# Bulk-load buffers moved to the front of SBUF, each row at a multiple of 512 bytes, in a one-token attention and MLP block

## Chip, cores, metric

One core of one Trainium2 chip. The metric is the device time of one execution in microseconds, as the median of several executions; a profile of one execution lies beside them.

## The reference

A decode step: layer norm of x, sliding-window attention over cached keys and values (8 KV heads, 4 query heads for each, window of 1024 keys, head size 128), an output projection, and a gated MLP branch.

```python
B, Sq, D = 4, 1, 512;  Hq, Hkv, Sk, Dh = 32, 8, 4096, 128;  F = 1792
W = min(4096, max(256, Sk // 4))                       # 1024 keys
q = (xn @ wq).reshape(B, Sq, Hq, Dh).transpose(0, 2, 1, 3)
k = repeat(k_cache[:, :, Sk - W:, :], 4, axis=1)       # v likewise
p = softmax(einsum("bhqd,bhkd->bhqk", q, k) * Dh ** -0.5)
s = einsum("bhqk,bhkd->bhqd", p, v).transpose(...).reshape(B, Sq, Hq * Dh) @ wo
g = silu(gelu(layernorm(xn) @ w1 + b1) @ w2 + b2)
return x + s * g
```

Everything that has to come from HBM (K and V windows, wq, wo, w1, w2) is 28.84 MB of bf16.

## The kernel before

All bulk loads are issued by SP (SyncE) on one DMA queue, queue 1 in the profile, in the order K0, K1, wq (two), K2 to K7, V0, w1, V1, w2, V2 to V7, wo (six pieces). The V loads reuse the K slots of kv_buf and wait for the transposes that read them. PE (TensorE) transposes K, computes scores, P times V, the MLP and the output projection as the loads land. The parts that matter here:

```python
sb = nc.alloc_sbuf_tensor              # buffers follow each other in this order, in steps of 32 B
x_bf = sb([4, 512], BF16)
x16 = sb([16, 128], BF16)
# ... some 20 small buffers cut ...
xyT = sb([128, 32], BF16)
wq_sb = sb([128, 4, HQ * DH], BF16)
qT = sb([128, 128], BF16)
w1_sb = sb([128, 4, F], BF16)
b1_sb = sb([1, F], BF16)
w2_sb = sb([128, FC, D], BF16)
b2_sb = sb([1, D], BF16)
wo_sb = sb([128, HKV, 4, D], BF16)
# ... cut ...
kv_buf = sb([128, NS, NC, DH], BF16)   # 8 slots of 8192 B per partition
kt_buf = sb([128, NKT, UT * 128], BF16)
P_buf = sb([128, HKV, NC * 16], BF16)

def load_v(g):
    d_v[g] = pg.dma("sp", "v%d" % g, lambda e: e.dma_start(
        kv_buf[:, (HKV + g) % NS, :, :].rearrange("p c d -> p (c d)"), cache_rows(A_v_cache, g)),
        t_last[(HKV + g) % NS] if HKV + g >= NS else None)

# the last work: the output projection, piece by piece as wo lands
def wo(k, rows):
    g0, g1, i0, i1, d = d_wo[k]
    # ... for g, i, c: matmul(psM[...], wo_sb[:, g, i, c*128:(c+1)*128], OW[:, i, g*4:(g+1)*4])
    return add("pe", fn, d, rows, mlp["g"])
```

The softmax here doesn't subtract the row's maximum and nothing guards it: scores larger than these inputs give would overflow.

Of the kernel before, what the change touches and what calls it, by code (L numbers as in the profile page):

```python
# [73 lines left out]
def bass_recurrent_scan__sliding_block_cached__mixer_channel_mlp__decode_kernel(  # L74
# [17 lines left out]
    BF16 = dt.bfloat16  # L92
    F32 = dt.float32

    B, D = 4, 512
    HQ, HKV, DH = 32, 8, 128
# [3 lines left out]
    F = B_w1.shape[1]  # L100
    FC = F // 128
    NC = 32
    KR = W // NC
    UT = 8
    NU = NC // UT
    NS = 8
    LAG = 8
    NKT = LAG + 2
# [5 lines left out]
    NEG = -30000.0  # L114

    sb = nc.alloc_sbuf_tensor
    x_bf = sb([4, 512], BF16)
    x16 = sb([16, 128], BF16)
    x32 = sb([4, 512], F32)
# [20 lines left out]
    negm = sb([128, 512], BF16)  # L140

    xyT = sb([128, 32], BF16)
    wq_sb = sb([128, 4, HQ * DH], BF16)
    qT = sb([128, 128], BF16)
    w1_sb = sb([128, 4, F], BF16)
    b1_sb = sb([1, F], BF16)
    w2_sb = sb([128, FC, D], BF16)
    b2_sb = sb([1, D], BF16)
    wo_sb = sb([128, HKV, 4, D], BF16)
    sel = sb([128, 4, 32], BF16)  # L150
    OW = sb([128, 4, HKV * 4], BF16)
    hT = sb([128, FC * 4], BF16)

    kv_buf = sb([128, NS, NC, DH], BF16)
    kt_buf = sb([128, NKT, UT * 128], BF16)
    P_buf = sb([128, HKV, NC * 16], BF16)
    OTb = sb([128, HKV * 16], BF16)
    den_sb = sb([128, HKV * 16], F32)
    rden = sb([128, HKV * 16], F32)
# [395 lines left out]
```

## Time and profile before

| | before |
|---|---|
| timed, median of the first 3 runs | 78.89 us (78.83 to 78.99) |
| the execution that was profiled | 77.54 us, span 75.8 us |
| bulk bytes, data packets | 28.84 MB, 3712 |
| busy: PE, VectorE, queue 1 | 74%, 45%, 91.6% of 16 engines |

A profile is read here from the slices (busy tenths in 40 equal parts), then in windows, then along the chain of work that ended last. The lines are in the prediction. Besides the views, I grouped the trace's records of single DMA packets (queue, start, duration, size); those tables are mine and stand in ordinary fences.

### The profile page before, as it was taken

What the parts mean: (1) busy time and instruction counts of PE and PEld (TensorE: products, weight loads), DVE (VectorE), ACT (ScalarE), POOL (GpSimd) and SP (SyncE); (2) the same over time, 40 slices, a digit from 0 to 9 for tenths busy, and PEclk for the clock granted to TensorE, in tenths of its full rate; (3) what the DMA queues carried; (4) which work ended last, traced back from release to release, by engine and by line L of the source; (5) the groups of instructions that cost most, each with busy time, mean ns of one, the idle gap of its engine ahead of it and who ended that gap; (6) DMA issues with size and microseconds to landing.
All of it is one profiled execution on the core that took longest, in us unless ns stands there. A gap on an engine that the chain in (4) does not pass through costs nothing.

```text
span 75.8 us, 2618 instructions
## 1 busy us (share of the span) xinstructions
PE 55.8 (74%) x1212; PEld 52.8 (70%) x1219; DVE 34.3 (45%) x81; ACT 8.4 (11%) x15; POOL 4.3 (6%) x12
## 2 busy tenths in 40 slices
PE   0009995003996989999999499999689979838850
PEld 0009994004995989999999399999489979737730
DVE  0788988000023668999999300000843563440010
ACT  0615200000000030330330351000100000000000
POOL 6970000000000000000000000000000000000000
PEclk9999999855555559999999995555555555555555
DMA  0899999999999999999999999999999999999600
GB/s 2 279 398 411 447 458 424 432 458 385 419 415 419 428 445 411 419 419 430 437 420 433 419 428 389 437 424 419 398 424 415 415 408 419 432 400 412 255 21 2
DMA packets 4214, 29.01 MB, mean 383 GB/s; under 512 B 486, under 2 KB 491, under 8 KB 1644
## 3 DMA queue, kind: packets, MB, share of 16 engines
q1 hardware_dynamic: 4160, 28.84, 91.6%
q8 instruction: 9, 0.15, 0.8%
q10 hardware_dynamic: 44, 0.01, 0.1%
q14 instruction: 1, 0.01, 0.0%
HBM read 28.85 MB, written 0.00 MB: 381 GB/s over the span
## 4 chain that ended last, share of the span: by engine, by line
DMA 44%; PE 31%; SPq 19%; issue 3%; DVE 1%
DMA wo_sb<-in_A_wo_dram 24%; DMA wq_sb<-in_A_wq_dram 20%; PE psK L272 18%; SPq L435 16%; PE psS L291 7%; PE psM L355 5%; SPq L201 2%; SPq L213 1%; PE psS L497 1%; PE psM L467 1%; SPq L206 0%; DVE o_bf L499 0%; DVE sg_sb L493 0%
## 5 line engine op out<-in xcount | busy, mean ns | idle before, releaser
L272 PE MATMUL psK<-ident,kv_buf 128*128 128x128 bf16 x256 | 23.1, 251 | 6.4 <-DMA kv_buf<-in_A_k_cache_dram 5.7
L272 PEld LDWEIGHTS psK<-ident,kv_buf 128*128 128x128 bf16 x256 | 18.7, 114 | 6.5 <-DMA kv_buf<-in_A_k_cache_dram 5.7
L278 DVE COPY kt_buf<-psK 128x1024 bf16<-128x1024 bf16 x32 | 21.1, 689 | 4.6 <-PE psK L272 4.5
L291 PE MATMUL psS<-qT,kt_buf 128*128 128x16 bf16 x256 | 10.6, 171 | 1.7 <-issue 1.4
L291 PEld LDWEIGHTS psS<-qT,kt_buf 128*128 128x128 bf16 x256 | 9.9, 99 | 2.4 <-issue 1.7
L309 PE MATMUL psO<-P_buf,kv_buf 128*128 128x16 bf16 x256 | 8.4, 175 | 0.5 <-issue 0.5
L309 PEld LDWEIGHTS psO<-P_buf,kv_buf 128*128 128x128 bf16 x256 | 8.1, 105 | 0.6 <-issue 0.6
L299 ACT ACTIVATE P_buf<-psS 128x512 bf16<-128x512 f32 x8 | 4.8, 597 | 32.9 <-PE psS L291 32.9
L355 PE MATMUL psM<-xyT,wq_sb 128*128 128x4 bf16 x128 | 3.5, 166 | 4.8 <-DMA wq_sb<-in_A_wq_dram 4.8
L355 PEld LDWEIGHTS psM<-xyT,wq_sb 128*128 128x128 bf16 x128 | 3.5, 104 | 4.8 <-issue 4.8
L373 PE MATMUL psM<-xyT,w_sb 128*128 128x4 bf16 x56 | 5.6, 204 | 0.0
L467 PE MATMUL psM<-OW,wo_sb 128*128 128x4 bf16 x128 | 4.4, 167 | 1.4 <-DMA wo_sb<-in_A_wo_dram 0.5
L467 PEld LDWEIGHTS psM<-OW,wo_sb 128*128 128x128 bf16 x128 | 3.9, 105 | 1.9 <-issue 0.9
L381 DVE TENSOR_SCALAR t_sb<-u_sb 128x56 f32<-128x56 f32 x1 | 0.2, 192 | 10.8 <-ACT u_sb L380 10.8
L318 PE MATMUL psO<-P_buf,ones_bf 128*128 128x128 bf16 x32 | 4.7, 302 | 0.0
L373 PEld LDWEIGHTS psM<-xyT,w_sb 128*128 128x128 bf16 x56 | 4.5, 154 | 0.2
L361 DVE CAST qT<-psM 128x128 bf16<-128x128 f32 x1 | 0.4, 440 | 8.2 <-PE psM L355 8.2
L327 DVE TENSOR_REDUCE den_sb<-psO 128x16 f32<-128x128 f32 x8 | 2.3, 289 | 3.5 <-PE psO L318 3.5
L375 PE MATMUL psM<-ones_bf,b_sb 1*128 1x4 bf16 x14 | 3.0, 215 | 0.0
L400 PE MATMUL psM<-hT,w_sb 128*128 128x4 bf16 x56 | 2.1, 167 | 1.0 <-DVE hT L392 1.0
L318 PEld LDWEIGHTS psO<-P_buf,ones_bf 128*128 128x128 bf16 x32 | 2.8, 128 | 0.0
L400 PEld LDWEIGHTS psM<-hT,w_sb 128*128 128x128 bf16 x56 | 1.8, 105 | 1.3 <-DVE hT L392 1.2
(57 smaller groups left out, 25.1 us busy)
## 6 DMA issues: line engine op xcount, KB each, us to landing
kv_buf<-in_A_k_cache_dram SPq DMA_DIRECT2D x8, 1024.0 KB, 21.5
kv_buf<-in_A_v_cache_dram SPq DMA_DIRECT2D x8, 1024.0 KB, 22.1
wq_sb<-in_A_wq_dram SPq DMA_DIRECT2D x2, 2048.0 KB, 13.2
w_sb<-in_B_w_dram SPq DMA_DIRECT2D x2, 1792.0 KB, 31.4
wo_sb<-in_A_wo_dram SPq DMA_DIRECT2D x3, 1024.0 KB, 24.7
wo_sb<-in_A_wo_dram SPq DMA_DIRECT2D x1, 512.0 KB, 21.6
wo_sb<-in_A_wo_dram SPq DMA_DIRECT2D x2, 256.0 KB, 18.0
x<-in_A_x_dram ACTq DMA_DIRECT2D x2, 2.0 KB
```

Of the source, the lines that this page charges most:

```text
L272: last = pe.transpose(psK[n % NB][:, j * 128:(j + 1) * 128], kv_buf[:, g, u * UT + j, :], ident[:, :])
L278: cp[n] = add("dve", lambda e: e.tensor_copy(kt_buf[:, n % NKT, :], psK[n % NB][:, 0:1024]), t, sc.get(n - NKT))
L291: last = pe.matmul(psS[g % 2][:, c * 16:(c + 1) * 16], kt_buf[:, n % NKT, j * 128:(j + 1) * 128], qT[:, g * 16:(g + 1) * 16], start=False, ...
L299: ex[g] = add("act", lambda e: e.activation(P_buf[:, g, :], psS[g % 2][:, 0:512], AF.Exp, scale=SCALE), sc[n])
L309: last = pe.matmul(pso[:, 0:16], kv_buf[:, (HKV + g) % NS, c, :], P_buf[:, g, c * 16:(c + 1) * 16], start=(c == 0), stop=(c == NC - 1))
L318: last = pe.matmul(pso[:, 128:256], ones_bf[:, :], P_buf[:, g, k * 128:(k + 1) * 128], start=(k == 0), stop=(k == 3))
L355: last = pe.matmul(psM[:, PS_Q + h * 4:PS_Q + (h + 1) * 4], wq_sb[:, c, h * DH:(h + 1) * DH], xyT[:, c * 4:(c + 1) * 4], start=(c == 0), s ...
L373: pe.matmul(o, bass.AP(w1_sb, c * F + k, [[4 * F, 128], [FC, 128]]), xyT[:, 16 + c * 4:16 + (c + 1) * 4], start=(c == 0), stop=False)
L375: last = pe.matmul(o, bass.AP(b1_sb, k, [[F, 1], [FC, 128]]), ones_bf[0:1, 0:4], start=False, stop=True)
L400: pe.matmul(o, w2_sb[:, k, c * 128:(c + 1) * 128], hT[:, k * 4:(k + 1) * 4], start=(k == 0), stop=False)
L435: e.dma_start(wo_sb[:, g0:g1, i0:i1, :], wo_r[:, g0:g1, i0:i1, :]))))
L467: last = pe.matmul(psM[:, PS_W + c * 4:PS_W + (c + 1) * 4], wo_sb[:, g, i, c * 128:(c + 1) * 128], OW[:, i, g * 4:(g + 1) * 4], start=firs ...
```

## The change

Its intent: rows that the bulk loads write should start on 512 B boundaries, in case the DMA engines write such rows faster. In the kernel before, kv_buf starts 384 B past such a boundary, w1, w2 and wo 256 B past, wq on it.

```diff
     sb = nc.alloc_sbuf_tensor
+    pad = sb([1, 192], BF16)
+    kv_buf = sb([128, NS, NC, DH], BF16)
+    wq_sb = sb([128, 4, HQ * DH], BF16)
+    wo_sb = sb([128, HKV, 4, D], BF16)
+    w1_sb = sb([128, 4, F], BF16)
+    w2_sb = sb([128, FC, D], BF16)
+    kt_buf = sb([128, NKT, UT * 128], BF16)
+    P_buf = sb([128, HKV, NC * 16], BF16)
     x_bf = sb([4, 512], BF16)
     # ... and the same seven lines removed further down
```

More of the change, by code (lines that the diff above doesn't have):

```diff
@@ L142, in bass_recurrent_scan__sliding_block_cached__mixer_channel_mlp__decode_kernel @@
     xyT = sb([128, 32], BF16)
-    wq_sb = sb([128, 4, HQ * DH], BF16)
     qT = sb([128, 128], BF16)
-    w1_sb = sb([128, 4, F], BF16)
     b1_sb = sb([1, F], BF16)
-    w2_sb = sb([128, FC, D], BF16)
     b2_sb = sb([1, D], BF16)
-    wo_sb = sb([128, HKV, 4, D], BF16)
     sel = sb([128, 4, 32], BF16)
@@ L152, in bass_recurrent_scan__sliding_block_cached__mixer_channel_mlp__decode_kernel @@
     hT = sb([128, FC * 4], BF16)
-    kv_buf = sb([128, NS, NC, DH], BF16)
-    kt_buf = sb([128, NKT, UT * 128], BF16)
-    P_buf = sb([128, HKV, NC * 16], BF16)
     OTb = sb([128, HKV * 16], BF16)
```

## The prediction

> **What bounds the kernel now.** I read the page's slices first, because moving buffers to other addresses can only act through transfers or through engines, and the slices say which of the two is full.
>
> ```profile
> PE   0009995003996989999999499999689979838850
> ...
> DVE  0788988000023668999999300000843563440010
> ...
> DMA  0899999999999999999999999999999999999600
> ...
> q1 hardware_dynamic: 4160, 28.84, 91.6%
> ```
>
> The 16 DMA engines are at 90% or more from the third slice to the 37th, while PE and DVE have holes. One queue carries practically everything: 28.84 MB in 4160 packets. Next I asked for the same in stretches of my own choice (columns: window, length, busy us of PE, PEld, DVE, ACT and POOL, granted clock, DMA share, GB/s):
>
> ```profile
> 8.00:18.00 10.00, 4.50 (x53) 4.24 (x50) 4.71 (x9) 0.01 (x1) 0.00 (x0) 0.83 0.99 423
> ...
> 24.00:35.00 11.00, 10.35 (x208) 10.16 (x211) 8.24 (x13) 1.79 (x3) 0.00 (x0) 0.80 1.02 427
> 35.00:48.00 13.00, 11.79 (x281) 11.30 (x281) 7.04 (x11) 2.99 (x5) 0.00 (x0) 0.90 1.00 420
> 48.00:62.00 14.00, 13.03 (x273) 12.32 (x274) 4.91 (x22) 0.65 (x3) 0.00 (x0) 0.50 1.01 419
> ```
>
> The DMA share is 0.99 to 1.02 whether PE is half idle (8 to 18) or nearly full. So PE's 90% in the later windows is work that keeps up, not the limit. The chain of waits in order of time then shows how the end is set:
>
> ```profile
> 42.90 2.22 SPq L435
> 45.12 0.04 issue
> 45.16 4.54 SPq L435
> ...
> 54.55 18.07 DMA wo_sb<-in_A_wo_dram
> 72.62 0.04 issue
> 72.67 0.39 PE psM L467 x8
> ```
>
> The last weight load is issued at 54.55 us and lands at 72.62 us: a 256 KB piece needs 18 us only because it stands behind others. The issues before it take 2 to 5 us each, which I read as a queue that is full and lets the issuer in only when room comes free. After the landing there are 8 matmuls, two small VectorE operations, one transpose and the store, about 3.2 us in all.
>
> The sum: the first bulk packet starts 2.22 us into the span, the bulk packets run over 70.03 us (first start to last end in the trace's records of single packets), and some 3.5 us follow: 75.8. The profiled run took 77.54 us as a whole, the timed ones 78.89 in the median. The question is therefore one: do these packets get shorter when they land on multiples of 512 bytes?
>
> [...]
>
> **The change part by part.** It removes and adds no instruction, wait or transfer; only addresses move, plus a 384-byte pad that nothing writes. The compiled program of before lists its addresses: wq starts at 28160 (55 x 512, already aligned), w1, w2 and wo at 256 past a multiple of 512, kv_buf at 127872, which is 384 past a multiple of 512 and 128 past one of 256. So of the 28.84 MB, wq's 4.19 MB are aligned already, w1, w2 and wo (7.86 MB) move from 256-aligned to 512-aligned, and only the caches (16.78 MB, 2048 rows of 8192 B) move from 128-aligned. After the change, working the allocation forward in steps of 32 B, the pad ends at 16896 (33 x 512), and kv_buf, wq, wo, w1, w2, kt_buf and P_buf follow, all multiples of 512 long. The small tensors come behind, at multiples of 32 as now.
>
> The kernel before thus holds its own experiment: packets of five sizes at three alignments. Median durations on queue 1 (my own grouping of the trace's packet records by size):
>
> - 2048 B (wo, 256 past): 84 ns, 256 packets
> - 4096 B (wo, 256 past): 159 ns, 896 packets
> - 8192 B (kv, 384 past): 309 ns, 2048 packets, mean 316.5
> - 14336 B (w1, w2, 256 past): 535 ns, 256 packets
> - 16384 B (wq, aligned): 611 ns, 256 packets
>
> First step, 512 against 256: the line through the 4096 and 14336 B packets has slope (535 - 159)/10240 = 0.03672 ns/B and gives 159 + 12288 x 0.03672 = 610.2 ns for 16384 B. The aligned wq packets take 611. Starting on 512 rather than 256 gains nothing.
>
> Second step, 256 against 128: the same line gives 159 + 4096 x 0.03672 = 309.4 ns for 8192 B. The kv packets, the misaligned ones, take 309. [...] The trace has -0.4 ns. So the penalty that the change sets out to remove is not there.
>
> Third step, the sum: 2048 packets x (309 - 309.4)/16 engines = 0.05 us, with the sign against the change, which is rounding. Cost of the moved engine operands: kt_buf goes from 128 past a multiple of 256 to a multiple of 512; its 32 copies take 669 to 693 ns now and I see no reason for another time. Expected change on the path that sets the end: 0.0 us.
>
> **The rivals.**
> - [...]
> - *The spread of the kv packets comes from the alignment.* Their mean is 7.5 ns above the median, 2048 x 7.5/16 = 0.96 us in all. If all of it went, 77.9 us, 1.2% faster. Against it: 1350 of the 2048 are exactly 309 ns, on the same addresses modulo 512. Single long packets (770 to 855 ns for kv) come every 6 us or so and also hit 14336 B packets (up to 1188) and 4096 B ones (up to 441), and packets of up to 656 ns stand at the start. Most of this looks like the memory side, which the change does not touch.
> - *An engine gets slower or faster at the new addresses.* The transposes release the V loads, and DVE's copies release the transposes (21.1 us busy in the page), so a slower copy could starve the queue. But the last V load is issued by 42.26 us, and loads issued then need some 20 us to land: this is the depth of the queue, hence the slack. A copy would have to become several 100 ns slower 32 times before it shows. A faster one gains nothing, since the queue is full. What lies on the path without cover is the tail of 3.2 us; 10% of it would be 0.3 us.
> - *Rows that straddle something at the new place.* All rows stay multiples of 2048 B; the order of the loads and their sources stay. I find nothing in the profile that speaks for it.
>
> **Range and chances.** The centre is the time of before, 78.9 us. Its own three runs span 0.2%, and the comparison of two sessions may add as much. [...] the tail could add or take 0.2 or 0.3. That gives 78.4 to 79.3 for 8 times in 10. Over 2% faster means under 77.3[...]: 0.015. Over 2% slower would need a mechanism that I do not know: 0.015. Within 2%: 0.97.
>
> **What would show it right or wrong.** Right: in the changed kernel the 8192 B packets keep a median of 309 ns (308 to 310), the other sizes theirs, the bulk transfers again run over 70.0 us give or take 0.4, the DMA share in the same windows stays at 0.99 to 1.02, the chain still ends in wo's last landing at 72.6 us give or take 0.5, and the copies into kt_buf stay near 690 ns. [...] the second as the same median with a mean near it. The third would show as holes in the DMA row after slice 10, with the issue of the V loads moved past 42 us. If the time moved by over 1% with all packet durations as now, my view that the packets' sum sets the time would be wrong.

What no trace or run of this case shows is cut from the record, each cut marked: a paragraph on what might make alignment matter, the first rival with its gain, and what rested on that gain. The sum came to 0.0 us of change on the path that sets the end, so to the 78.9 us of before. The range of 78.4 to 79.3 us and the 0.015 for over 2% faster counted the first rival's gain as one more term. Two readings are guesses that no trace shows: the full queue that lets the issuer in (measured are issues of 2.22 to 4.54 us, and landings some 20 us later), and "the memory side".

## The result

| | before | changed |
|---|---|---|
| median of 4 runs | 78.91 us (78.83 to 78.99) | 78.53 us (78.38 to 78.58) |
| profiled execution | 77.54 us, span 75.8 us | 78.50 us, span 76.8 us |

The ratio is 0.9949, with a 95% interval of 0.9931 to 0.9967: within 2%, but clear of noise. A ratio is the mean time of one kernel's fast runs over the mean of the other's fast runs of the same rounds, so it is not quite the ratio of the medians. The instruction streams of the two kernels are the same but for addresses.

Two things did not fit together at first. The timed runs got shorter, while the profiled span got longer by 1.0 us. And the profiled execution of before, at 77.54 us, is far from its own timed runs. From the page of the changed kernel, the DMA row of its slices and its queues:

```profile
DMA  0899999999999999999999999999999999998200
...
q1 hardware_dynamic: 4160, 28.84, 90.2%
q8 instruction: 9, 0.15, 0.7%
```

Two of the windows that the prediction shows of before, now of the changed kernel (same columns):

```profile
8.00:18.00 10.00, 4.41 (x53) 4.15 (x51) 4.71 (x9) 0.01 (x1) 0.00 (x0) 0.82 0.99 420
...
48.00:62.00 14.00, 12.78 (x293) 12.12 (x294) 5.59 (x24) 0.65 (x3) 0.00 (x0) 0.50 1.01 422
```

The end of its chain of waits:

```profile
54.38 19.21 DMA wo_sb<-in_A_wo_dram
73.59 0.05 issue
73.64 0.39 PE psM L471 x8
```

The body is the same: the DMA share in the windows is 0.99 and 1.01 as before. The end differs: the last weight piece now takes 19.21 us from issue to landing, where it took 18.07. Windows over the last microseconds show how. Of the kernel before:

```profile
71.00:72.00 1.00, 0.76 (x23) 0.59 (x21) 0.00 (x0) 0.00 (x0) 0.00 (x0) 0.50 0.55 213
72.00:73.00 1.00, 0.68 (x16) 0.55 (x16) 0.00 (x0) 0.00 (x0) 0.00 (x0) 0.50 0.13 43
```

And of the changed kernel:

```profile
71.00:72.00 1.00, 0.59 (x16) 0.51 (x16) 0.00 (x0) 0.00 (x0) 0.00 (x0) 0.50 0.41 148
72.00:73.00 1.00, 0.00 (x0) 0.00 (x0) 0.00 (x0) 0.00 (x0) 0.00 (x0) 0.50 0.06 20
73.00:74.00 1.00, 0.74 (x16) 0.59 (x16) 0.00 (x0) 0.00 (x0) 0.00 (x0) 0.50 0.01 4
```

In the changed kernel less is left to move after 71 us (148 against 213 GB/s), so the transfers were ahead. But from 72 to 73 us a share of 0.06, which is one engine's worth of 16, still moves data while PE does nothing at all (x0) and waits for it. The packet records suggest the reason:

```
changed kernel, end of the trace (start us, duration ns, size B):
queue 8 (instruction fetch)  70.595   961  16384
queue 1 (wo)                 71.541   232   2048
                             71.759   227   2048
                             71.972   228   2048
                             72.185   132   2048
                             72.313    84   2048
                             ... one packet every 80 ns ...
                             73.119    84   2048   <- last
before: last instruction fetch at 72.232; last bulk packets of the engines end by 72.253,
        each 2048 B packet takes 84 ns
```

Queue 8, whose kind the page gives as "instruction", fetches instructions: 9 packets of 16384 B in mid-run, 5.8 to 7.1 us apart. In the changed kernel the ninth comes at 70.6 us, before the weights are through. Three wo packets right behind it take 227 to 232 ns instead of 84, and after 72.3 us one packet follows another, every 80 ns, which I read as a single engine working off its share. In the profiled execution of before the ninth fetch came at 72.23 us, just as the packets ended.

The second finding is in the durations of the 2048 cache packets:

```
8192 B packets          before   changed
median, ns                 309       309
mean, ns                 316.5     314.7
exactly 309 ns            1350      1874
310 to 330 ns              635       107
longer than 330 ns          61        63
mean of the 9 instruction fetches, ns   1030   931
```

The median did not move. The spread of 1 to 21 ns above it is nearly gone. The 60 or so long ones remain: they are the start of the run and the packets that run into an instruction fetch (before: fetches at 21.93, 28.09, 34.24, 40.99 us; long 8192 B packets of 773 to 855 ns at 22.93, 29.15, 35.32, 41.99 us).

From this came theories to test, each with a letter. **A**: the spread and the longer fetches come from rows off a boundary, and removing them is the gain. **F**: an execution ends with its last DMA engine, and whether the ninth fetch hits an engine that still has packets to write makes a step of over a microsecond. Rivals: **P**, place and order of the buffers; **N**, chance from build to build; **R**, another cause of the step.

### The profile page after: what moved, and what is told of

Its sections match the earlier page's. It is cut to its first block, busy times and chain, and to the rows that moved or that the text cites. A ratio compares the mean times of both kernels' runs of the same rounds, so it can differ in the third digit from the quotient of the medians.

```text
span 76.8 us, 2625 instructions
## 1 busy us (share of the span) xinstructions
PE 56.2 (73%) x1219; PEld 52.6 (68%) x1219; DVE 34.2 (45%) x81; ACT 8.4 (11%) x15; POOL 4.3 (6%) x12
## 3 DMA queue, kind: packets, MB, share of 16 engines
q1 hardware_dynamic: 4160, 28.84, 90.2%
## 4 chain that ended last, share of the span: by engine, by line
DMA 45%; PE 31%; SPq 19%; issue 1%; DVE 1%
DMA wo_sb<-in_A_wo_dram 25%; DMA wq_sb<-in_A_wq_dram 20%; PE psK L276 17%; SPq L439 16%; PE psS L295 6%; PE psM L359 5%; PE psS L291 2%; SPq L205 2%; SPq L217 1%; PE psS L501 1%; PE psM L471 1%; SPq L210 0%; DVE o_bf L503 0%; DVE sg_sb L497 0%
## 5 line engine op out<-in xcount | busy, mean ns | idle before, releaser
L291 PE MATMUL psS<-negm,ind 128*128 128x512 bf16 x8 | 3.5, 442 | 0.0
```

The source lines that it names most:

```text
L291: pe.matmul(psS[g % 2][:, 0:512], ind[:, :], negm[:, :], start=True, stop=False, skip_group_check=True)
```

## The experiments

Twelve builds ran; those of one call share the runs of before. The record marks all twelve as correct, also the three whose results are wrong, so this mark vouches for little. "Extended packets" below are the data packets, from 8 us into the span on, that are 2 to 21 ns over the common duration for their size (309, 535, 611, 159 and 84 ns for 8192, 14336, 16384, 4096 and 2048 B); the microseconds beside them are what packets up to 21 ns over add up to, divided by 16 engines. There are about 3440 packets in this stretch.

### First call: which bytes, and is it chance?

**before_again**, no edit.

> The kernel before, unchanged, timed against itself: what a second build and another place in the round make of the time, and a second profile. Theory A (alignment of the caches' rows trims a small spread of 2 to 20 ns off the 8192 B packets): ratio 1.000 within 0.2%, and again some 600 to 700 of the 2048 cache packets between 310 and 330 ns. Theory N (the spread and the 0.5% differ from run to run or from build to build, whatever the layout): a ratio off 1 by up to 0.5%, or a count of such packets far from 635, say under 250. In both: the profiled run of before at 77.5 us was an exception against its timed 78.9, so this profile should show a span near 77.2 us, with an instruction fetch on a DMA engine shortly before the last bulk packet.

Measured: 77.65, 79.01, 79.03, 77.60, 77.43, 78.77 us; the 11 runs of before beside it: 77.54 to 77.75 (5 runs) and 78.80 to 79.11 (6 runs). **The kernel has two levels**, 1.3 us apart, with nothing between. The granted clock is the same in both (0.70 to 0.74), so this is not a clocked-down state, although runs over 1.5% above the fastest are labelled slow. From here on I compare level with level. Over all sessions 26 of 56 runs of before are low (mean 77.60) and 30 high (mean 78.95). The first session happened to time before in the high level only. The profile is of a low run: span 75.9, fetch at 72.25 us; I had expected 77.2, wrongly. No run of before on its high level was ever profiled: what its ninth fetch does there is inferred from the other kernels. 565 extended packets, 0.211 us per engine (before: 578, 0.217). The spread repeats, so N falls for the spread.

**kv_only**

```diff
+    pad = sb([1, 64], BF16)
     kv_buf = sb([128, NS, NC, DH], BF16)
```

> The kernel before with one pad of 128 bytes ahead of kv_buf: the caches, kt_buf and P_buf start on multiples of 512, wq as before too, w1, w2 and wo stay 256 past, the small tensors stay in front. Theory A (the caches' rows off a 256 B boundary cost): the whole gain, ratio 0.993 to 0.997, and 50 to 200 cache packets of 310 to 330 ns. Theory P (it is the place and order of the buffers, or w1, w2 and wo on 512): ratio 1.000 within 0.2% and a count near 635. Theory N: no order in it.

Measured: six runs of 78.33 to 78.86 us, mean 78.70, all in the high level; the reported ratio of 1.0133 (1.0102 to 1.0164) sets them against before's low runs alone. Against the high runs of the same call (mean 78.94) they are 0.24 us faster. 28 extended packets, 0.013 us; fetches 931 ns in the mean. So 128 bytes ahead of kv_buf do to the packets all that the whole change does, w1, w2 and wo still being 256 past a multiple of 512. P falls for the packets. The ninth fetch is at 71.01 us and the last bulk packet ends at 73.38: the step is there.

**off128** and **off32**

```diff
-    pad = sb([1, 192], BF16)
+    pad = sb([1, 192 + 64], BF16)      # off128; off32 has 192 + 16
```

> The changed kernel with the pad 128 bytes longer: the order of the change, but every bulk buffer 128 past a multiple of 512. Theory A: no gain is left, ratio 0.999 to 1.005, the spread is back, now on the other sizes of packets too. [...] Theory P (order): ratio near 0.995 as with the change. Theory N: anything.

> The changed kernel with the pad 32 bytes longer: every bulk buffer 32 past a multiple of 512, so off 64 and 256 too. Theory A: at least as slow as with 128 past, ratio 1.000 to 1.010, the spread on all sizes. [...] Theory P: ratio near 0.995.

Measured, off128: 78.06 to 78.23 us (4 runs) and 79.59 to 79.75 us (3 runs), two levels again, 0.5 and 0.7 us above those of before; ratio of the low ones 1.0064 (1.0041 to 1.0087). 1549 extended packets, 0.612 us. Off32: six runs of 79.66 to 80.00 us, 0.9 us above before's high level; ratio against its low runs 1.0277 (1.0254 to 1.0301). 2510 extended packets, 0.890 us. The mean fetch took 1069 and 1072 ns. The order of the buffers is that of the change in both, so P falls for the time as well, and A holds with a graded answer:

| start of the cache rows | extended packets | us per engine | mean fetch, ns |
|---|---|---|---|
| 0 past 512 (changed) | 23 | 0.010 | 931 |
| 256 past (off256, below) | 14 | 0.009 | 933 |
| 384 past, only the caches off 256 (before) | 578 | 0.217 | 1030 |
| 128 past, all bulk buffers (off128) | 1549 | 0.612 | 1069 |
| 32 past, all bulk buffers (off32) | 2510 | 0.890 | 1072 |

The medians moved by 0 to 3 ns: off128's are 311, 538, 611, 160 and 84 ns, against common durations of 309, 535, 611, 159 and 84.

### Second call: is it the fetch, and is 256 enough?

**after_again**, the changed kernel with no edit.

> The changed kernel, unchanged, once more, beside the next three. Theory F: each run's time is set by the last of the 16 DMA engines, and the two levels of the kernel before (77.4 to 77.75 and 78.8 to 79.1 us) differ by whether the ninth instruction fetch hits an engine that still has weight packets to write. In the changed kernel the ninth fetch comes at 70.6 us, before the packets end, in every run: one level, 78.3 to 78.6 us, no run under 78. Rival R (the two levels have another cause, such as the chip): two levels here too, some runs near 77.2.

Measured: 78.57, 78.64, 78.73, 78.75 us, one level; before 77.55 to 77.68 (6 runs) and 78.85 to 79.03 (5). Taken against before's low runs the change is 1.38% *slower* (ratio 1.0138, 1.0123 to 1.0153), against its high runs (mean 78.97) 0.4% faster. The level matters more than the change. The fetch is at 70.70 us, the last packet at 73.23, as in the first profile.

**after_lag2** and **before_lag2**

```diff
-    LAG = 8
-    NKT = LAG + 2
+    LAG = 2
+    NKT = 10
```

> The changed kernel with 2 instead of 8 groups of transposes ahead of the query projection (kt_buf keeps its size), so that PE reaches a given instruction later and the chain of instruction fetches starts some 1.3 us later. Theory F: the ninth fetch comes at 71.9 us or later and misses the bulk packets in most runs: 77.0 to 77.3 us, 1.3 to 1.5 us under the changed kernel. If the shift is just too small, two levels, 77.1 and 78.5. Rival R, or a kernel bound by PE: no gain, or slower since transposes move into PE's busy stretch (78.5 to 80).

> The kernel before with the same 2 instead of 8. Theory F: its low level alone, 77.4 to 77.8 us. Against it the changed kernel with the same edit then shows what the alignment is worth without the fetch in the way: theory A says 0.2 to 0.5 us less, that is 0.3 to 0.6%. Rival R: two levels as before.

Measured: after_lag2 77.19, 77.25, 77.38, 77.98, 78.22, 78.59 us; before_lag2 77.97, 78.58, 78.66, 78.73, 78.98, 79.02 us. In the profiled low run of after_lag2 the fetch came at 71.89 us and the packets ended at 71.98: the changed layout can reach 77.2, which none of its 8 unedited runs did. But the spread of the times and before_lag2 missed what I expected. The chain of waits shows why: PE has become the bound at the end. Of after_lag2:

```profile
68.53 0.70 PE psM L471 x21
...
69.57 3.13 PE psM L471 x107
```

And of before_lag2:

```profile
70.19 0.70 PE psM L467 x21
...
71.14 3.03 PE psM L467 x107
```

107 of the 128 output matmuls run in one go, behind weights that had already landed; in the chain of the changed kernel only the last 8 stood there. So this pair supports F by its fastest runs only, and says nothing clean on A. PE is also 1.6 us later in before's layout with the same instructions; its seventh fetch is at 62.61 instead of 60.99 us. That late instructions hold PE up is my guess; it was not shown.

**off256**

```diff
-    pad = sb([1, 192], BF16)
+    pad = sb([1, 192 + 128], BF16)
```

> The changed kernel with the pad 256 bytes longer: every bulk buffer 256 past a multiple of 512. Theory A with the boundary at 256 B: the same as the changed kernel within 0.2%, and under 60 packets of any size that are 2 to 21 ns over the common duration after 8 us. If 512 is what matters: a spread between that of the changed kernel and that with 128 past, and 0.3% or more slower than the changed kernel.

Measured: 77.26 us once, 78.50 to 78.69 us five times (mean 78.56; the changed kernel beside it 78.67). 14 extended packets, 0.009 us. Rows 256 past are as good here as rows on 512 (23 extended packets, 0.010 us). The profile is of the run at 77.26 us, so it shows this layout on the low level. Its last windows:

```profile
71.00:72.00 1.00, 0.83 (x24) 0.75 (x24) 0.00 (x0) 0.00 (x0) 0.00 (x0) 0.50 0.53 195
72.00:73.00 1.00, 0.51 (x14) 0.34 (x10) 0.19 (x1) 0.00 (x0) 0.00 (x0) 0.50 0.00 0
```

The end of its chain of waits:

```profile
54.41 17.93 DMA wo_sb<-in_A_wo_dram
72.34 0.05 issue
72.39 0.39 PE psM L471 x8
```

The fetch is at 71.96 us, the last packet ends at 72.02; the DMA share after 72 us is 0.00, and wo's last piece is in at 72.34 instead of 73.59 us. This is the same layout as the changed kernel as far as packets go, with the step away.

### Third call: the step taken away on purpose

**fewer_after** and **fewer_before**: 144 of PE's weight-load and matmul pairs left out, in the changed kernel and in the one before. The results are wrong; all transfers are the same.

```diff
-            for c in range(4):                  # query projection; the first MLP layer likewise
+            for c in range(2):
-                for k in range(FC):             # second MLP layer
+                for k in range(FC // 2):
-            for k in range(4):                  # denominator
+            for k in range(1):
```

> The changed kernel with 144 weight-load and matmul pairs left out of PE (half of the query projection's and the MLP's contractions, three of four matmuls of each denominator); wrong result on purpose, all transfers as they were. PE's stream is 288 instructions shorter[...]. Theory F: the ninth fetch is gone or comes after the bulk packets, no DMA engine is hit twice, one level at 77.0 to 77.4 us, no run over 77.6. Rival R (two levels or the 78.5 have another cause): 78.4 to 78.7 in most runs, since the 28.84 MB are the same.

> The kernel before with the same 144 pairs left out; wrong result on purpose. Theory F: one level at 77.4 to 77.75 us, the low one of before. Against the run above it gives what the alignment alone is worth: theory A 0.2 to 0.5 us, from 0.21 us of small extra time per DMA engine and the shorter fetches (0.93 against 1.05 us). If the alignment is worth nothing: the same time within 0.1 us.

Measured: fewer_after 77.11 to 77.20 us in six runs, fewer_before 77.56 to 77.65 us in six runs, while before itself had both levels beside them (77.54 to 77.78, 7 runs; 78.85 to 79.02, 6 runs). Both have **one level, the low one**, with the same 28.84 MB. The queues on the page of fewer_after:

```profile
q1 hardware_dynamic: 4160, 28.84, 91.7%
q8 instruction: 8, 0.13, 0.6%
```

and the end of its chain of waits:

```profile
54.26 18.00 DMA wo_sb<-in_A_wo_dram
72.26 0.05 issue
72.31 0.39 PE psM L471 x8
```

Eight fetches instead of nine, the last at 69.46 us, and wo is in at 72.26 us. That PE has an eighth less to do (49.2 instead of 56.2 us busy) is not the cause: fewer_before takes what before takes on its low level (ratio 1.0000, 0.9986 to 1.0014). R falls, and F holds in that the ninth fetch makes the step (77.16 us in the mean with eight fetches, 78.67 with nine in after_again); that the last DMA engine sets the end is inferred below.

One part of F needs putting right. The eighth fetch of fewer_after, at 69.46 us, also hit an engine with weights to write: four 2048 B packets behind it took 211 to 232 ns. Yet there is no step. The number of bulk packets in flight suggests why. In the changed kernel it is 16 at 70.25 us, 8 from 70.75 to 71.50, and 1 from 72.00 until the end at 73.20. In fewer_after it is 15 at 70.00, 9 or 8 from 70.75 to 71.50, and 0 after 71.95. This fits eight fetches on eight different engines, which end some 1.4 us behind the other eight, and a ninth on an engine that has had one already. The records don't name the engine of a packet, so this is inferred. The lengths of the fetches fit it: in after_again 961, 962, 947, 886, 886, 942, 931 and 921 ns, then 960 again.

The pair also gives the change alone, with no step in the way: means 77.16 against 77.58, 0.43 us or 0.55%. In the records the bulk packets end at 71.95 against 72.39 us, 0.44 us. Of this the extended packets are 0.211 us (0.003 against 0.214 us per engine) and the shorter fetches 0.09 us, if an engine has one each (930 against 1023 ns). The rest, some 0.13 us, lies in the first 8 us, where packets were over their common durations by 0.49 and 0.63 us per engine. Over all profiles of full kernels that start-up figure scatters from 0.16 to 0.58 us without order by layout, so that part stays open.

**bare32**: the layout of off32, transfers only. The output is x, wrong. Attention and MLP are gone; PE runs one burst and VectorE another.

```diff
+    def burst(pe):
+        for j in range(160):
+            last = pe.transpose(psK[...], ones_bf[:, :], ident[:, :])
+    t_b = add("pe", burst, d_k[3], c_id)
+    for n in range(24):                 # after d_v[2]
+        add("dve", lambda e: e.tensor_copy(kt_buf[:, n % NKT, :], psK[n % NB][:, 0:1024]), ...)
```

> The transfers alone with every bulk buffer 32 bytes past a multiple of 512; no attention, no MLP, the output is x, wrong on purpose. PE makes one burst of 160 transposes of constants after the fourth K load, VectorE 24 copies from PSUM after the third V load, nothing else reads or writes SBUF meanwhile. Theory C (the extra 2 to 21 ns of a misaligned packet arise only where an engine uses SBUF at the same time): under 10% of the packets extended outside the bursts, 80% or more in the burst of PE or in that of VectorE, which tells whose accesses they are. Theory S (a misaligned row costs by itself[...]): 80% or more extended throughout. In both the bulk packets end near 71 us, since no PE instructions are fetched in mid-run.

Measured: 76.96 us (one run), last bulk packet at 72.70 us, not 71 as I had expected. Its last windows:

```profile
71.00:72.00 1.00, 0.00 (x0) 0.00 (x0) 0.00 (x0) 0.00 (x0) 0.00 (x0) 0.50 0.24 86
72.00:73.00 1.00, 0.00 (x0) 0.00 (x0) 0.00 (x0) 0.00 (x0) 0.00 (x0) 0.50 0.04 16
```

At 71.00 us 16 bulk packets are in flight, at 71.50 two, from 71.75 to 72.70 a single one. The only fetch on queue 8 came at 32.63 us; I had expected none in mid-run. So one engine seems to end 1.2 us behind the rest. That would fit the reading above, if it is the engine of this fetch; the records don't show which it is.

Other windows of this kernel (columns as above) mark what ran when, and extended packets were counted in such stretches:

```profile
8.00:18.00 10.00, 0.00 (x0) 0.00 (x0) 0.00 (x0) 0.00 (x0) 0.00 (x0) 1.00 1.00 426
...
24.00:29.00 5.00, 5.00 (x65) 5.00 (x64) 0.00 (x0) 0.00 (x0) 0.00 (x0) 1.00 1.01 419
...
40.00:50.00 10.00, 0.00 (x0) 0.00 (x0) 0.00 (x0) 0.00 (x0) 0.00 (x0) 0.50 1.01 424
```

```
stretch us    what runs      extended packets
 8 to 16.5    nothing          5 of 224   (all wq, 16384 B)
17 to 20      nothing         32 of 142
20 to 23      nothing        104 of 157
24 to 34      PE             472 of 508
36 to 50      nothing        524 of 557
51 to 67      VectorE        938 of 1114
```

With no engine at work 94% of the packets are extended (36 to 50 us), as with PE at work. Theory C, that engines at work on SBUF cause it, falls: no engine has to be at work for a row off the boundary to cost. But it is not a constant cost either, which S wanted: the wq packets are free of it (5 of 224 here, 6 of 223 in off32, 3 of 224 in off128), and it grows from nothing to full between 17 and 24 us. The size of the packets alone doesn't decide. In off128 all 285 of the 8192 B packets that start from 17 to 23 us take exactly 309 ns; from 26 to 36 us, at the same offset, 293 of 455 are extended. In before it even comes and goes: 128 of 242 from 30 to 36 us, 34 of 333 from 36 to 50 us, while the rows of w1 and w2, on multiples of 256 B, pass between them, and 344 of 509 from 50 to 60 us. What decides stays open.

### Fourth call: a version to beat both

**lean**: the changed kernel, 30 pairs fewer on PE, correct.

```diff
-            for k in range(4):   # denominator, N = 128 each
+            pe.matmul(pso[:, 128:512], ones_bf[:, :], P_buf[:, g, 0:384], start=True, stop=False, ...)
+            last = pe.matmul(pso[:, 128:256], ones_bf[:, :], P_buf[:, g, 384:512], start=False, stop=True, ...)
-                last = pe.matmul(o, bass.AP(b1_sb, ...), ones_bf[0:1, 0:4], ...)   # 14 of them
+        add("dve", lambda e: e.tensor_tensor(h_sb, psM[...], b1 broadcast over the batch, ALU.add))
```

> A correct version meant to beat both: the changed kernel with 30 pairs fewer on PE (each denominator in two matmuls of 384 and 128 columns instead of four of 128; b1 added by VectorE instead of by 14 one-row matmuls). Theory F: 60 instructions fewer move the point at which the ninth fetch is asked for some 30 weight loads later into the output projection, 1.3 to 2.5 us, so that it comes at 71.9 us or later: 77.0 to 77.4 us in most runs, about 0.5% under the low level of before and 1.8% under its high one. If the shift is too small or b1's 28-byte rows cost, two levels, 77.2 and 78.5, or 78.5 throughout. Correct result.

Measured: 77.83, 77.90, 78.06, 78.78, 79.23, 79.37 us; before beside it 77.48 to 77.66 (5 runs) and 78.82 to 79.32 (6). A miss. The ninth fetch did move, to 72.45 us, but the packets ended late too, at 72.53 us. Queue 10 has 186 packets instead of 44, since b1 now comes in 128 short rows, and two runs are at or above before's high level. No correct version beat both kernels.

## Why the prediction was right, and where its steps were not

The range held: 78.53 us lies in 78.4 to 79.3, and "within 2%" came true. By its steps:

- **What bounds the kernel** was right in kind: the DMA engines are full, and neither PE nor VectorE sets the end. It was incomplete in one point. The end is set by the last packets, which look like those of one engine of 16, not by the sum of packets. One instruction fetch of 0.96 us and three packets slowed by 0.14 us each are 1.4 us, which is the distance of the two levels (78.95 - 77.60 = 1.35). As the packets in flight suggest (a single one from 72.00 to 73.20 us), they fall on one engine, and count because that engine had carried a fetch before. I had read the 77.54 of the profile beside the 78.89 of the timed runs and passed over it; it was the sign of the two levels.
- **First step, 512 against 256**: right. Off256 has 14 extended packets, the changed kernel 23.
- **Second step, 128 against 256**: right on the median (309 ns in both), wrong in the conclusion "the penalty is not there". A median cannot see a third of the packets moving by 2 to 20 ns.
- **Third step, the sum**: this is the term that was mis-sized. It said 0.05 us, from medians; the change is worth 0.4 us at equal level (0.43 in the pair without the step). The means, 316.5 and 314.7 ns, would have been the right thing to multiply: 2048 x 1.8/16 = 0.23 us.
- **The second rival** had the right place: "The spread of the kv packets comes from the alignment", 0.96 us if all of it went. I set it aside because 1350 packets were exactly 309 ns at the same address modulo 512, and called the long ones the memory side. In fact the spread has two parts: the small one, some 0.2 us, is the alignment; the long ones every 6 us (773 to 855 ns, 0.46 to 0.55 us over the common 309) stand right behind instruction fetches, which the page lists as queue 8 and which I had not matched in time.
- What the runs show of rows off a boundary: with all of them 128 past, the medians rose by 0 to 3 ns, and the 8192 B packets got 3.0 ns longer in the mean; with 32 past, 4.9 ns. The 16384 B packets, all through before 18 us, got 0.1 and 0.2 ns longer.
- **Engines at new addresses**: right; the copies into kt_buf take 689 ns in the mean in both profiles.
- **Landing of wo at 72.6 us give or take 0.5**: missed, 73.59 us, by the fetch. The bulk transfers ran over 71.0 us (2.21 to 73.20), outside the 70.0 give or take 0.4, for the same reason. By the prediction's own sign for its third rival one would have looked for holes after slice 10; there are none. The loss is behind the last slice that is full.

Had the first session met before on its low level, the same kernel would have read as 1.4% slower, and a range of this width around 77.6 us would have missed the 78.5. That is also the prediction's own last sign: over 1% moved with the median durations as before, so the sum of the packets does not set the time. The number came out right partly by luck, through the level that was timed.

## What to carry to other kernels

Where transfers fill the time, look at the last DMA engine and at what else it carries: one instruction fetch more, the ninth, on what looks like one engine, cost 1.4 us here, three times what the layout was worth, and leaving out 288 PE instructions removed it (8 fetches, 77.16 us in the mean, in fewer_after). It cost nothing where it came as the last packets ended (off256: fetch at 71.96 us, last packet at 72.02, 77.26 us). Multiply mean packet durations, not medians, when small penalties are in question, and try rows of bulk buffers that start on 256 B (14 extended packets with 256 past here, 1549 with 128 past); a pad of 128 bytes ahead of one buffer did as much to the packets as the whole reordering (28 extended packets against 23). When a kernel's runs fall into two levels, compare level with level and say how many runs are in each, or a change of 0.5% will read as anything from +1.4% to -0.5%.
